# A two-layer attention and feed-forward kernel on one core: the feed-forward's first products leave PSUM through a 16-bit copy, and the order of segments and queries changes

## Chip, cores and metric

The kernel runs on one core of one Trainium2 chip. The time is device microseconds of one execution. The core has a matrix engine (TensorE, PE in the profile; its weight loads are PEld), a vector engine (VectorE, DVE), an activation engine (ScalarE, ACT), a general engine (GpSimd, POOL) and an engine that here only issues DMAs (SyncE, SP). Each engine works through its own instructions in the order in which the program lists them; semaphores hold an instruction until what it needs is done.

## The reference

```python
def _A_ref(x, wqkv, wo):            # B, S, D = 1, 2048, 512; H = 32 heads of 16
    qkv = (x @ wqkv).reshape(B, S, 3, H, Dh).transpose(2, 0, 3, 1, 4)
    q, k, v = qkv[0], qkv[1], qkv[2]
    p = _softmax(einsum("bhqd,bhkd->bhqk", q, k) * Dh ** -0.5, axis=-1)
    o = einsum("bhqk,bhkd->bhqd", p, v)
    return o.transpose(0, 2, 1, 3).reshape(B, S, D) @ wo

def _B_ref(x, w1, w2):              # w1 512 x 1792, w2 1792 x 512
    return silu(x @ w1) @ w2

x = x + _A_ref(_layernorm(x), A_wqkv, A_wo)
x = x + _B_ref(_layernorm(x), B_w1, B_w2)
x = x + _A_ref(_layernorm(x), A_wqkv, A_wo)      # the same weights again
x = x + _B_ref(_layernorm(x), B_w1, B_w2)
```

All tensors are bfloat16. The 2 x 32 softmaxes over 2048 x 2048 scores hold most of the work.

## The kernel before

**Tiles.** A layer's attention is cut into segments: a chunk c of 512 queries (4 chunks) by a head block hb of 4 heads (8 blocks). A segment of kind "all" goes over 16 key tiles of 128 keys, with two score tiles per key tile (a pair of heads each, 128 keys x 2 x 512 queries), 2048 score tiles in the whole program. In layer 1 the first segments are split: "old" segments take the first 12 key tiles, as the last chunk of layer 0 is not ready yet, and "new" segments the last 4; their partial sums are joined with a factor exp of the difference of the two shifts (`f_piece`, L465 and L468).

**A score tile's way.** TensorE makes it (L1209) in one of three PSUM slots of 1024 columns. Then one of two routes is taken. ScalarE applies the exponential (L1424, one instruction of 128 x 1024) and writes a bf16 buffer; one row for the value product. Or VectorE makes the bit pattern of a power of two by one multiply and add (L1454), and three further shifted versions of it come from integer adds, mostly on GpSimd (L1515), some on VectorE (L1488); the four together make four rows for the value product, whose sum stands for the exponential. TensorE multiplies rows with the values (L1285) into one PSUM bank per segment. A ones column beside the values gives the softmax's denominator. The row buffers are 11 tiles of its own and tiles lent from other tensors while these are idle: 12 more at the start, of which the last goes back at segment 32, and 12 again from segment 59.

**Side work.** Keys, queries, values, output projection, feed-forward and layer norms are "pieces": lists of steps (engine, planned ns, function, marks). All products of pieces go through one PSUM bank (tag "g", `narrow`). The mark "o" on a step opens that bank, "c" closes it: until the closing step's planned end no other piece may open it. "l" marks VectorE steps that are planned around GpSimd's running instruction (`self.lock`). Key pieces: 4 matmuls (L282, each as four column groups), copy (L291). Query pieces: 4 matmuls, copy (L359), absolute value (L366), bound times key maximum (L374), one matmul, sum (L383). The first product of the feed-forward, for each of 14 blocks of 128 hidden columns in each of 7 chunks: 4 matmuls into the bank, tanh of half of it on ScalarE into an fp32 tile (L545, `h_tanh`), and `(tanh + 1) * product` on VectorE with the product read from PSUM (L549, `h_out`), which closes the bank. Then four second products of 14 matmuls each, and the sum with x (L558). The eighth chunk's feed-forward is in `ending`, after the last segment, written out by hand.

**The planner.** `Flow` runs when the program is built. It keeps a planned time for each engine, takes the turn of the engine that is earliest, and lists the next instruction there; the order of all engines is so fixed before the run. `segs` is the order of segments. `musts(i)` gives what has to be made while segment i runs (`prep` of segment i+1 up to `n_old` = 41, of i+2 from there on), `due` gives it a due tile, `pace` a rate of credit that side pieces spend. `self.cur` is the one piece that holds the bank; `self.bg` are steps behind, which VectorE takes when it is free. `want_dve` decides whether VectorE gets a score tile: it needs, among other conditions, `SPARE` free row buffers beyond those owed, and not too many shifts waiting. `MANY` is the number of waiting row pairs above which value products go ahead of side work. `warm` lists idle matmuls (L1320) where TensorE has nothing else. `heads_piece` transposes a finished segment's output by DMA on the SP queue, two head blocks to a normalisation (L479, L480), one where it stands alone.

Of the kernel before, what the change touches and what calls it, by code (L numbers as in the profile page):

```python
# [20 lines left out]
def kernel(  # L21
# [10 lines left out]
    nc = tc.nc  # L32
# [25 lines left out]
    ) / 128  # L58
    BASE = 128 * (127 - MEAN)

    OLD = 3 * TT // 4
    MM, T_TANH, T_ISSUE, T_LAND, T_POOL = 217, 478, 1450, 2700, 2500
    NB = 11
# [168 lines left out]
    def pe(ns, fn, g=""):  # L232
        return ("pe", ns, fn, g)
# [218 lines left out]
    def f_piece(seg, after):  # L452

        cell = {}

        def a():
            cell["ps"] = narrow("f_ps")
            mm(cell["ps"][:, :], sel[:, 0, :], seg.QT, True, False)

        def b():  # L460
            mm(cell["ps"][:, :], sel[:, 1, :], q_kept(seg), False, True)

        def e():
            cell["f"] = tpool.tile([P, 512], FP32, name="f_sb", tag="t")
            nc.scalar.activation(cell["f"][:], cell["ps"][:, :], ACT.Exp, scale=float(SCALE))  # L465

        def m():
            nc.vector.tensor_tensor(  # L468
                out=o_kept(seg), in0=o_kept(seg), in1=cell["f"][:], op=ALU.mult
            )  # L470
            seg.scaled = True

        return Piece([pe(MM, a, "o"), pe(MM, b), act(T_TANH, e, "c"), dve(690, m, "l")], after)


    def heads_norm(at_ps, hb, attn):
# [10 lines left out]
    at_cell = {}  # L487

    def heads_piece(oT, seg, attn):
        alone = seg.L == 1 and (seg.c < 2 or (seg.c == NQC - 1 and seg.hb == HB - 2))  # L490
        k = 0 if alone else seg.hb % 2
        if k == 0:
            at_cell["at"] = opool.tile([P, 4, 2, P], BF16, name="at", tag="at")
        at = at_cell["at"]
        turn(at[:, :, k, :], oT[:])
        if not alone and k == 0:
            return None
        n = 4 * (k + 1)
        heads = at[:].rearrange("p t s (j w) -> p t (s j) w", j=4)[:, :, 0:n, :]
        return Piece([dve(640 if k == 0 else 920, lambda: heads_norm(heads, seg.hb - k, attn))])  # L500
# [64 lines left out]
    def ffn_pieces(c, emit_out, ln, after):  # L565
        cell = ln
        pieces = ln_pieces(c, ln, after)
        for ft in range(FT):
            hc = {}

            def a(ft=ft, hc=hc):
                bank(hc, "h_ps")

            def d(hc=hc):
                hc["t"] = h_tanh(hc["ps"][:, :])

            def e(ft=ft, hc=hc):
                h_out(cell["hT"], ft, hc["ps"][:, :], hc["t"])

            pieces.append(Piece(  # L580
                four(lambda cts, ft=ft, hc=hc: h_mm(c, ft, hc["ps"][:, :], cts), a)
                + [act(T_TANH, d), dve(690, e, "c")],
                pieces[1] if ft == 0 else None,
            ))
        for tq in range(4):
            yc = {}

            def ya(ft, tq=tq, yc=yc):
                if ft == 0:
                    bank(yc, "y2_ps")  # L590
                y_mm(cell["hT"], tq, yc["ps"][:, :], (ft,))

            def yb(tq=tq, yc=yc):
                y_out(4 * c + tq, yc["ps"][:, :], emit_out)

            pieces.append(Piece(
                [pe(MM, lambda ft=ft, ya=ya: ya(ft), "" if ft else "o") for ft in range(FT)]
                + [dve(690, yb, "c")] + ([] if emit_out else [stats_step(ln, c, tq)])
            ))
        return pieces  # L600

# [149 lines left out]
            self.opened = [False, False]  # L751

    segs = [Seg(0, c, hb, "all") for c in range(NQC) for hb in range(HB)]
    segs += [Seg(1, 0, hb, "old") for hb in range(HB)]
    segs += [Seg(1, 1, hb, "old") for hb in MORE]
    for hb in range(HB // 2):
# [18 lines left out]
        return pieces  # L775

    period = [c for c in range(NQC) for _ in range(HB)]
    period += [NQC] * (HB + len(MORE)) + [NQC + 1] * (2 * HB) + [NQC + 2] * (2 * HB)

    def ns_of(pieces):  # L780
# [48 lines left out]

    def musts(i):  # L830

        ts = list(range(i + 1 if i <= n_old else i + 2, i + 2 if i < n_old else i + 3))
        if (segs[i].L, segs[i].c) == (0, NQC - 2):
            ts.append(i + HB)
        last = (NQC - 1) * HB
        return [
            p for t in ts if t < len(segs) and not (last <= t < last + HB and t != i + HB)
            for p in due(prep(t), first[t])
        ]
# [59 lines left out]
    class Flow:  # L899

        def __init__(self):
            self.pe = self.act = self.dve = self.pool = self.sp = self.end = 0.0
            self.lock = self.held_port = 0.0
            self.mode = ""
            self.n = 0
            self.slots = [wide("slot") for _ in range(3)]
            self.free = [0.0] * 3
            self.held = [None] * 3
            self.exps = []
            self.zs = []  # L910
            self.passes = []
            self.lanes = [[], []]
            self.bufs = [(0.0, b) for b in bufs]
            self.retired = []
            self.qs = [[], [], [], []]
            self.cur = None
            self.bg = []
            self.g = 0.0
            self.credit = self.rate = 0.0
            self.open = 0  # L920
            self.o_ps = q_ps
            self.o_free = 0.0
            self.close_at = None
            self.last_dve = -9
            self.started = -1
            self.lost = 0.0
            self.runs = []
            self.heads = None
            self.chain = None
            self.units = [(tq, k) for tq in range(4) for k in range(CT)]  # L930
            self.kept = []
            self.turned = None
            self.log = {}
# [52 lines left out]
        def ready(self, p):  # L986
            at = p.ready
            if p.chain is not None and self.chain is not None and p.chain is not self.chain:
                return None
            for d in p.after:  # L990
                if not d.done:
                    return None
                at = max(at, d.ready)
            if "o" in p.steps[0][3]:
                at = max(at, self.g)
            return at

        def step(self, p, at):

            engine, ns, fn, g = p.steps.pop(0)  # L1000
            if not p.begun and p not in self.bg:
                self.cur = p
                for q in self.qs:
                    if p in q:
                        q.remove(p)
# [22 lines left out]
            fn()  # L1028
            if p.steps:
                p.land = max(p.land, self.landed(end))  # L1030
            if g == "c":
                self.g = end + 50
                self.cur = None
                if p.steps:
                    self.bg.append(p)
            if p.steps:
                p.ready = end + lat[("pe", "dve", "act").index(p.steps[0][0])]
            else:
                p.done = True
                if p.chain is not None and p.chain["last"] is p:  # L1040
                    self.chain = None
                p.ready = max(p.land, self.landed(end), end + 50 + p.lag)
                if p in self.bg:
                    self.bg.remove(p)
# [1 line left out]
        def front(self, pieces):  # L1046
            self.qs[0][:0] = pieces

        def background(self):
            return next((p for p in self.bg if self.ready(p) is not None), None)  # L1050

        def force(self, piece):
            while not piece.done:
                self.head()
                p = self.cur or self.background()
                if p is None:
                    q = next(q for q in self.qs if piece in q)
                    p = q[0]
                    if self.chain is not None and p.chain not in (None, self.chain):
                        self.force(self.chain["last"])  # L1060
                        continue
                    if p.steps[0][0] == "sp" or self.ready(p) is None:
                        self.force(next(d for d in p.after if not d.done))
                        continue
                at = self.ready(p)
                self.step(p, max(at, getattr(self, p.steps[0][0])))
# [340 lines left out]
        def act_turn(self):  # L1407
            t = self.act
            p = self.head()
            if p is not None and p.steps[0][0] == "act" and p.ready <= t + 150:  # L1410
                self.step(p, max(t, p.ready))
                return True
            if not self.exps:
# [125 lines left out]
    SWITCH, T_PASS, T_BITS, T_SHIFT = 100, 1225, 430, 1000  # L1539
    HELP, WAIT = 2, 100  # L1540

    LAST, BEHIND, SPARE, ROWS, LATE, EVEN = 5, 3, 5, 20, 900, 0
    SPAN, WARM, FEW, MANY = 3300, 0.65, 2, 8
    TAU, NEAR, URGENT, HARD = 700, 300, 4000, 6000
    FROM, TO, EARLY = 0, 99, 300
    EARLIER = 12
    HOT = 0.9
    MOST = 2600

    ordered = {  # L1550
# [153 lines left out]
```

## Time and profile before

| | us |
|---|---|
| median of 3 runs | 1661.9 (1661.09 to 1665.58) |
| the profiled execution's own time | 1662.01 |
| its span, first to last instruction | 1660.1 |
| granted TensorE clock, mean | 0.991 |
| busy: PE, ACT, POOL, DVE | 1576.4, 1592.1, 1220.3, 1152.4 |

The span is what the profile shows; 1.9 us of the execution lie around it. Busy time of an engine is the union of its instructions' spans. ScalarE's and TensorE's instructions overlap with their successors, so a mean duration there is longer than the distance from one start to the next. A group's row gives count, busy us, mean ns, then the idle time of that engine just before the group's instructions and what ended it.

### The profile page before, as it was taken

To read this page: it belongs to the slowest core of one execution; us is meant where nothing else is said; L and a number is where in the kernel's file an instruction comes from. 1 tells how busy PE (TensorE), PEld (TensorE's weight loads), DVE (VectorE), ACT (ScalarE), POOL (GpSimd) and SP (SyncE) were. 2 spreads that over 40 slices of the span, in tenths; PEclk is the share of its full clock that TensorE was granted. 3 is DMA by queue.
4 is the path that set the end of the run, shared out by engine and by line. 5 is a ranking of instruction groups with operands and counts; after the bars stand their busy time and mean duration, and the time that the engine had idled before them with its cause. 6 is when DMAs were issued, how large, how long until landed. Compare 5 with 4: busy or idle time off the path is not lost.

```text
span 1660.1 us, 42534 instructions
## 1 busy us (share of the span) xinstructions
PE 1576.4 (95%) x17499; PEld 503.8 (30%) x17505; DVE 1152.4 (69%) x1461; ACT 1592.1 (96%) x1805; POOL 1220.3 (74%) x1296
## 2 busy tenths in 40 slices
PE   7999999999999999999999998999999999999998
PEld 3232322233323333233232233222223222332333
DVE  6678779777877666656885557876665677687654
ACT  5899999999999999999999998999999999999993
POOL 2699998888788767767676655886567889788770
PEclk9999999999999999999999999998999999999999
DMA  5000000001000001000000000001000100010010
GB/s 190 5 8 8 5 20 21 8 5 21 21 21 5 8 21 30 8 8 18 21 14 2 2 14 8 11 11 30 17 8 11 27 21 8 15 36 8 11 24 13
DMA packets 83683, 30.79 MB, mean 19 GB/s; under 512 B 75552, under 2 KB 82464, under 8 KB 83488
## 3 DMA queue, kind: packets, MB, share of 16 engines
q1 hardware_dynamic: 82000, 26.10, 6.6%
q8 instruction: 137, 2.24, 0.6%
q10 hardware_dynamic: 1488, 1.97, 0.4%
q14 instruction: 58, 0.48, 0.1%
HBM read 7.86 MB, written 2.10 MB: 6 GB/s over the span
## 4 chain that ended last, share of the span: by engine, by line
PE 62%; ACT 21%; DVE 10%; issue 4%; POOL 1%; DMA 1%; ACTq 0%; DVEq 0%; POOLq 0%
PE slot L1209 21%; PE q_ps L1285 18%; ACT p L1424 13%; PE y_ps L282 7%; PE q_ps L282 4%; ACT v L1424 3%; PE k_ps L282 3%; PE h_ps L282 3%; ACT t_sb L545 3%; DVE p L1454 2%; DVE hT L549 1%; PE v_ps L282 1%; ACT q_old L1424 1%; PE q_ps L1320 1%; DVE attn L480 1%
## 5 line engine op out<-in xcount | busy, mean ns | idle before, releaser
L1424 ACT ACTIVATE p<-slot 128x1024 bf16<-128x1024 f32 x1173 | 1177.8, 1203 | 22.0 <-PE slot L1209 18.7
L1515 POOL TENSOR_TENSOR p<-p,steps 128x512 int32<-128x512 int32 x564 | 590.5, 1069 | 256.6 <-DVE p L1454 206.3
L1285 PE MATMUL q_ps<-p,v 128*17 128x512 bf16 x4594 | 532.8, 385 | 4.8 <-DVE p L1454 2.0
L1209 PE MATMUL slot<-QT,KT 32*128 32x512 bf16 x3104 | 443.0, 384 | 26.0 <-ACT p L1424 12.4
L1454 DVE TENSOR_SCALAR p<-slot 128x1024 uint16<-128x1024 f32 x280 | 341.6, 1220 | 127.0 <-PE slot L1209 119.8
L1209 PEld LDWEIGHTS <-KT 32*128 32x128 bf16 x4096 | 189.5, 91 | 587.1 <-issue 582.3
L1424 ACT ACTIVATE v<-slot 128x1024 bf16<-128x1024 f32 x306 | 350.6, 1233 | 2.0 <-PE slot L1209 2.0
L1285 PEld LDWEIGHTS <-v 128*17 128x17 bf16 x6586 | 165.8, 89 | 281.8 <-issue 223.5
L1285 PE MATMUL q_ps<-v,v 128*17 128x512 bf16 x1304 | 200.5, 381 | 1.9 <-DVE oT L1113 0.9
L1515 POOL TENSOR_TENSOR p<-v,steps 128x512 int32<-128x512 int32 x158 | 166.0, 1068 | 34.0 <-DVE v L1454 34.0
L1454 DVE TENSOR_SCALAR v<-slot 128x1024 uint16<-128x1024 f32 x99 | 121.0, 1222 | 66.0 <-PE slot L1209 62.8
L1515 POOL TENSOR_TENSOR v<-p,steps 128x512 int32<-128x512 int32 x133 | 141.1, 1068 | 30.6 <-DVE p L1454 27.2
L1424 ACT ACTIVATE q_old<-slot 128x1024 bf16<-128x1024 f32 x127 | 150.5, 1225 | 1.3 <-PE slot L1209 1.3
L282 PE MATMUL h_ps<-xnT,w_sb 128*32 128x512 bf16 x1568 | 130.5, 384 | 14.0 <-DVE hT L549 11.8
L1209 PE MATMUL slot<-q_old,KT 32*128 32x512 bf16 x896 | 121.3, 382 | 5.5 <-ACT p L1424 4.8
L549 DVE SCALAR_TENSOR_TENSOR hT<-t_sb,h_ps 128x512 bf16<-128x512 f32 x98 | 67.0, 684 | 79.0 <-ACT t_sb L545 79.0
L282 PE MATMUL y_ps<-w_sb,hT 128*32 128x512 bf16 x1568 | 119.4, 383 | 0.9 <-DVE qc L359 0.3
L1285 PE MATMUL q_ps<-q_old,v 128*17 128x512 bf16 x578 | 99.5, 381 | 0.5 <-DVE oT L1113 0.2
L282 PE MATMUL q_ps<-xnT,wkq 128*32 128x512 bf16 x1008 | 84.7, 384 | 2.9 <-DVE hT L549 1.2
L282 PE MATMUL k_ps<-xnT,wkq 128*32 128x512 bf16 x960 | 80.5, 388 | 2.5 <-DVE KT L291 1.4
L1515 POOL TENSOR_TENSOR q_old<-p,steps 128x512 int32<-128x512 int32 x67 | 72.2, 1085 | 11.4 <-DVE p L1454 11.2
L1515 POOL TENSOR_TENSOR v<-v,steps 128x512 int32<-128x512 int32 x63 | 67.3, 1075 | 13.4 <-DVE v L1454 12.2
(162 smaller groups left out, 1512.3 us busy)
## 6 DMA issues: line engine op xcount, KB each, us to landing
w_sb<-in_B_w_dram SPq DMA_DIRECT2D x2, 1792.0 KB, 14.7
out_dram<-x_sb SPq DMA_DIRECT2D x15, 128.0 KB, 1.7
x_sb<-in_A_x_dram SPq DMA_DIRECT2D x3, 512.0 KB, 10.3
wraw<-in_A_wqkv_dram ACTq DMA_DIRECT2D x1, 1024.0 KB, 8.4
at<-oT SPq DMA_TRANSPOSE x63, 2.3
xnT<-hT SPq DMA_TRANSPOSE x44, 2.3
wv_sb<-in_A_wqkv_dram ACTq DMA_DIRECT2D x1, 512.0 KB, 10.7
wo_sb<-in_A_wo_dram SPq DMA_DIRECT2D x1, 512.0 KB, 11.3
```

Of the source, the lines that this page charges most:

```text
L282: nc.tensor.matmul(ps[g, :], lhsT=lhsT[:, g], rhs=rhs, start=start, stop=stop, skip_group_check=True)
L480: nc.vector.tensor_tensor(out=attn[:, :, 64 * hb : 64 * hb + DH * n].rearrange("p t (j d) -> p t j d", j=n), in0=at_ps[:, :, :, 0:DH], in1 ...
L545: nc.scalar.activation(t_sb, ps, ACT.Tanh, scale=0.5)
L549: nc.vector.scalar_tensor_tensor(out=hT[:, ft, :], in0=t_sb, scalar=1.0, in1=ps, op0=ALU.add, op1=ALU.mult)
L1209: nc.tensor.matmul(self.slots[k][:, jj, :], lhsT=KT[32 * j : 32 * j + KR, t.seg.hb, t.kt * P : (t.kt + 1) * P], rhs=t.seg.QT[32 * j : 32 * ...
L1285: nc.tensor.matmul(self.o_ps[32 * j : 32 * j + VW, :], lhsT=vs[seg.L][:, t.kt, 4 * seg.hb + j, :], rhs=buf[:, jj, :], start=not seg.opened ...
L1320: nc.tensor.matmul(out[0:DH, :], lhsT=wkq[rows, 0, 2 * D : 2 * D + DH], rhs=wo_sb[rows, 0, :], start=out is not self.o_ps, stop=out is not ...
L1424: nc.scalar.activation(buf[:].rearrange("p a b -> p (a b)"), self.slots[x.slot][:].rearrange("p a b -> p (a b)"), ACT.Exp, scale=float(SCALE),
L1454: nc.vector.tensor_scalar(out=whole.bitcast(U16), in0=self.slots[x.slot][:].rearrange("p a b -> p (a b)"), scalar1=float(UNIT), scalar2=fl ...
L1515: nc.gpsimd.tensor_tensor(out=b1.bitcast(I32), in0=b0.bitcast(I32), in1=steps32[:, k : k + 1].to_broadcast([P, 512]), op=ALU.add,)
```

## The change

The feed-forward's product in the seven planned chunks goes from PSUM to SBUF by a VectorE copy into its place in `hT` (bf16), which closes the bank; tanh and product read that copy, the product writes over it in place. Tanh and product are now background steps, with a mark "t" so that one tanh tile is in use at a time, and ScalarE's turn looks among background steps. The second products wait for all fourteen first ones. Segment (chunk 1, head block 0) moves to second place, behind (chunk 0, head block 0); the heads of blocks 0 and 1 of chunks 0 and 1 are normalised alone. From segment 16 on queries are prepared two segments ahead. `SPARE` goes from 5 to 4 and `MANY` from 8 to 6. The ending keeps its own order and reads PSUM as before.

```diff
-        return Piece([pe(MM, a, "o"), pe(MM, b), act(T_TANH, e, "c"), dve(690, m, "l")], after)
+        return Piece([pe(MM, a, "o"), pe(MM, b), act(T_TANH, e, "ct"), dve(690, m, "l")], after)
...
-        alone = seg.L == 1 and (seg.c < 2 or (seg.c == NQC - 1 and seg.hb == HB - 2))
+        alone = seg.c < 2 and (seg.L == 1 or seg.hb < 2)
+        alone = alone or (seg.L, seg.c, seg.hb) == (1, NQC - 1, HB - 2)
...
-            def d(hc=hc):
-                hc["t"] = h_tanh(hc["ps"][:, :])
+            def w(ft=ft, hc=hc):
+                nc.vector.tensor_copy(out=cell["hT"][:, ft, :], in_=hc["ps"][:, :])
+
+            def d(ft=ft, hc=hc):
+                hc["t"] = h_tanh(cell["hT"][:, ft, :])
 
             def e(ft=ft, hc=hc):
-                h_out(cell["hT"], ft, hc["ps"][:, :], hc["t"])
+                h_out(cell["hT"], ft, cell["hT"][:, ft, :], hc["t"])
 
             pieces.append(Piece(
                 four(lambda cts, ft=ft, hc=hc: h_mm(c, ft, hc["ps"][:, :], cts), a)
-                + [act(T_TANH, d), dve(690, e, "c")],
+                + [dve(690, w, "c"), act(T_TANH, d, "t"), dve(T_PROD, e)],
                 pieces[1] if ft == 0 else None,
             ))
+        hs = pieces[2:]
...
-                + [dve(690, yb, "c")] + ([] if emit_out else [stats_step(ln, c, tq)])
+                + [dve(690, yb, "c")] + ([] if emit_out else [stats_step(ln, c, tq)]), hs
             ))
...
     segs = [Seg(0, c, hb, "all") for c in range(NQC) for hb in range(HB)]
+    segs.insert(1, segs.pop(HB))
...
     period = [c for c in range(NQC) for _ in range(HB)]
+    period[HB] = 0
...
     def musts(i):
 
-        ts = list(range(i + 1 if i <= n_old else i + 2, i + 2 if i < n_old else i + 3))
+        ts = [i + 1] * (i <= AHEAD) + [i + 2] * (i >= AHEAD)
+        if n_old < AHEAD + HB * 5 and n_old - 2 <= i <= n_old + 1:
+            ts = {n_old - 2: [n_old], n_old - 1: [], n_old: [n_old + 1], n_old + 1: [n_old + 2, n_old + 3]}[i]
...
+            if "t" in p.steps[0][3] and self.t_user is not None:
+                return None
...
+            if "t" in g:
+                self.t_user = p
...
-            if g == "c":
+            if "c" in g:
...
                 p.done = True
+                if self.t_user is p:
+                    self.t_user = None
...
-        def background(self):
-            return next((p for p in self.bg if self.ready(p) is not None), None)
+        def background(self, engines=("dve",)):
+            able = [p for p in self.bg if p.steps[0][0] in engines and self.ready(p) is not None]
+            now = [p for p in able if self.ready(p) <= getattr(self, p.steps[0][0]) + 150]
+            return now[0] if now else min(able, key=self.ready, default=None)
...
-                p = self.cur or self.background()
+                p = self.cur or self.background(("dve", "act"))
...
-            if p is not None and p.steps[0][0] == "act" and p.ready <= t + 150:
+            if p is None or p.steps[0][0] != "act" or self.ready(p) is None:
+                p = self.background(("act",))
+            if p is not None and p.ready <= t + 150:
...
-    LAST, BEHIND, SPARE, ROWS, LATE, EVEN = 5, 3, 5, 20, 900, 0
-    SPAN, WARM, FEW, MANY = 3300, 0.65, 2, 8
+    LAST, BEHIND, SPARE, ROWS, LATE, EVEN = 5, 3, 4, 20, 900, 0
+    SPAN, WARM, FEW, MANY = 3300, 0.65, 2, 6
...
+    AHEAD = 16
+    T_PROD = 690
```

More of the change, by code (lines that the diff above doesn't have):

```diff
@@ L1039, in step @@
                 p.done = True
+                if self.t_user is p:
+                    self.t_user = None
                 if p.chain is not None and p.chain["last"] is p:
@@ L1547 @@
     HOT = 0.9
+    AHEAD = 16
+    T_PROD = 690
     MOST = 2600
```

## The prediction

> **What bounds the kernel now.** I began with the page's header, busy shares and slices, to find the engine that never pauses.
>
> ```profile
> span 1660.1 us, 42534 instructions
> PE 1576.4 (95%) x17499; PEld 503.8 (30%) x17505; DVE 1152.4 (69%) x1461; ACT 1592.1 (96%) x1805; POOL 1220.3 (74%) x1296
> ACT  5899999999999999999999998999999999999993
> ```
>
> Two engines stand near the full span. ScalarE (ACT) is below 9 in four slices only: the first, the last, the second (41 to 83 us) and the 25th (996 to 1037 us). The matmul share is less telling, for single matmuls of 384 ns overlap, and the groups hold filler (181 of L1320 into q_ps alone), which the scheduler adds only where TensorE has nothing else. So the sum is made on ScalarE. Next came the groups, for the price of each operation.
>
> ```profile
> L1424 ACT ACTIVATE p<-slot 128x1024 bf16<-128x1024 f32 x1173 | 1177.8, 1203 | 22.0 <-PE slot L1209 18.7
> L545 ACT ACTIVATE t_sb<-h_ps 128x512 f32<-128x512 f32 x98 | 74.5, 760 | 0.0
> L549 DVE SCALAR_TENSOR_TENSOR hT<-t_sb,h_ps 128x512 bf16<-128x512 f32 x98 | 67.0, 684 | 79.0 <-ACT t_sb L545 79.0
> L468 DVE TENSOR_TENSOR v<-v,f_sb 128x512 f32<-128x512 f32 x8 | 9.6, 1194 | 4.2 <-ACT f_sb L465 4.2
> ```
>
> The four tile names of L1424 (p, v, q_old, idle) sum to 1173 + 306 + 127 + 27 = 1633 exponentials; the other 415 of the 2048 score tiles go to VectorE (L1454: 280 + 99 + 30 + 6). ScalarE's operations overlap, so the price of one is start to start. In the timeline eight exponentials fill 429.45 to 436.77 us: 0.91 us each. A tanh starts at 501.67 and the next exponential at 502.15: 0.48 us. Then 1633 x 0.91 + 98 x 0.48 + 10 rescaling exponentials x 0.48 = 1538 us, against 1580 us from the first exponential (37.6) to the end of the last one's turn (about 1617). Some 42 us are gaps; 43 us lie behind the last one, in the ending, which is not touched.
>
> Then the timeline, for where the gaps are. The largest:
>
> ```profile
> 65.28 0.29 DVE L374 TENSOR_SCALAR bm<-E,amax 128x128 bf16<-128x128 f32 x1
> 66.55 0.40 PE L282 MATMUL q_ps<-qu,bm 128*32 128x512 bf16 x4
> 67.00 0.69 DVE L383 TENSOR_TENSOR QT<-q_ps,qc 128x512 bf16<-128x512 f32 x1 [1.44 <-PE q_ps L282]
> 67.74 0.61 PE L1209 MATMUL slot<-QT,KT 32*128 32x512 bf16 x6 [0.79 <-DVE QT L383]
> 68.17 2.86 ACT L1424 ACTIVATE p<-slot 128x1024 bf16<-128x1024 f32 x3 [5.73 <-PE slot L1209]
> ```
>
> ScalarE idles 5.73 us at the end of the first segment: scores of the second need its query QT, which needs the key maximum of head block 1, whose last key copy ends at 64.3. Within 37 to 76 us the excess over the usual spacing is 9.8 us. A second cluster lies at 985 to 1161 us, where the new keys of the second layer arrive: 18 gaps, 15 us together, the longest 1.9. Elsewhere there is next to nothing: from 93 to 565 us ScalarE is busy 470.66 of 472 us.
>
> Last, VectorE's share of the exponentials by stage, and the waits around the bank that the change frees:
>
> ```profile
> 93.00:565.00 472.00, 173.19 (x142) 1.00 0.06 13
> 565.00:1008.00 443.00, 118.51 (x97) 1.00 0.06 13
> 1233.00:1594.00 361.00, 129.44 (x106) 1.00 0.08 18
> ```
>
> ```profile
> DVE hT L549 <- ACT t_sb L545: 79.0, 65, 2.7
> PE h_ps L282 <- DVE hT L549: 11.8, 29, 0.7
> ```
>
> VectorE takes 0.30, 0.22 and 0.29 tiles per us. The weak middle is where the lent buffers have gone back (14, then 12 and 11 tiles instead of 23). The single projection bank costs TensorE 11.8 us of waits behind the feed-forward product, never over 0.7 at a time, in stretches where ScalarE does not stop.
>
> **The change, part by part.**
>
> *Order of segments.* Segment 1 becomes (chunk 1, head block 0), whose keys exist; it needs one query (4 matmuls of one piece, four VectorE steps). Head block 1's keys get all of segment 1, where 84 column matmuls fitted into 25 us before. Of the 9.8 us I keep the first 0.95 (start-up) and some 0.8 for a new boundary: -8. Bounds -10 and -4 (the key chain is late for segment 2 instead). The two heads left unpaired add two normalisations of 0.86 + 0.25 us in place of half of two of 1.13 + 0.35: about 1.5 us of VectorE, hidden. Their transposes on SP are as many as before.
>
> *Freeing the bank.* A copy ends the hold of the bank, before it lasted over the tanh's turn on ScalarE and the product. By the waits above this gives ScalarE nothing: 0 by itself. It lets the feed-forward of chunk 3 end sooner, ahead of 985 to 1161; with the queries there re-timed I take -3 of those 15 us, bounds -8 and +3 (segment 43's query is now queued a segment later). The second products wait for all 14 first ones: up to a tanh's turn (0.9 + 0.48) and a product (1.2) per chunk, 2.6 x 7 = 18 us in the feed-forward's own queue; other queues' pieces fill TensorE, and ScalarE waits only where a due time is missed: 0.
>
> *Queries two segments ahead from segment 16.* Between segments 16 and 40 boundaries show no gap over 1.3 us, most none: 0.
>
> *SPARE 5 to 4, MANY 8 to 6.* One buffer less is held back when VectorE is offered a tile. From 14 buffers (418 to 565 us: 39 tiles, 0.265 per us) to 11 or 12 (0.22) the rate falls by about 0.02 per us for one buffer. Over the 700 us that are short of buffers (418 to 1008 and 1151 to 1260) this would be 14 tiles x 0.91 = 13 us. The reserve was also there for ScalarE's own buffers, so I take half: -7, bounds -14 and +2. MANY works on long lists of waiting rows, which 11 buffers do not hold: 0.
>
> *VectorE's added work.* 98 copies from PSUM at 0.69 (as L341, 691 ns) = 68 us. The product now has both inputs in SBUF. The rows nearest to it are L468 and L480, also with two:
>
> ```profile
> 1019.22 3.21 POOL L1515 TENSOR_TENSOR p<-p,steps 128x512 int32<-128x512 int32 x3 [4.76 <-DVE p L1454]
> 1021.45 1.52 DVE L468 TENSOR_TENSOR v<-v,f_sb 128x512 f32<-128x512 f32 x1
> ```
>
> GpSimd's running shift ends at 1022.43, and VectorE's operation 0.54 us after that: it had waited 0.98. All ten of L468 last as long as the running shift has left, and about 0.55 more. So a product costs about 1.19 instead of 0.684, 98 x 0.5 = 50 us more, and the scheduler counts it as 690 ns without a turn on the port. Together VectorE gains 118 us, 69% to 76%. The cover is its idle time, 31% of the span. Where that fails, a tile goes back to ScalarE. Bounds 0 and +19 (a quarter of the 118 displaces tiles of 1.22 + 0.2 us: 21 x 0.91); I take +5. Queued behind a late product stand key and query copies and passes that free score slots. From 93 to 565 us many VectorE operations already wait for GpSimd (L366 lasts 735 ns on the mean, 278 at the least) and ScalarE lost 1.3 us: +3, bounds 0 and +10.
>
> *The tanh's source*, SBUF in 16 bits instead of PSUM. No wide ScalarE operation here reads SBUF. Of its 0.48 us, 0.43 go with the 512 elements (0.91 less 0.48); the fixed 0.05 might vanish or double: 98 x 0.05 = 5 us either way; I take 0, as both rows have the same fixed part. [...]
>
> Sum: -8 - 3 - 7 + 5 + 3 = -10 us. The profiled execution took 1662.0 us (span 1660.1 and 1.9 around it), the median of the runs is 1661.9: forecast 1652.
>
> **The rivals.**
>
> *VectorE pays in tiles (slower), 0.21.* In the feed-forward segments of the buffer-rich stages (273 to 350, 1329 to 1426) VectorE is 78 and 75% busy and GpSimd 86 and 89%; up to five products and copies add 5 x 1.19 = 6 us to 24. If a quarter of the 118 us displaces tiles, +19, and the spare buffer then brings nothing; with -8 - 3 it is +8: 1670. It turns slower where displaced work passes a seventh (11 of 76 us). For it: the product's price is underrated by the scheduler. Against: 28 of the 98 products fall between 565 and 1008 us, where VectorE is 65% busy.
>
> *Gain and price cancel, 0.16.* The start's 8 us come, the tanh from SBUF (+5) and the delays (+3) take them back, tiles stay: 1662.
>
> *Buffers were the bound, 0.19.* The middle's rate rises half-way, to 0.26: 0.04 x 443 = 18 tiles there, 5 in other short stretches, 23 x 0.91 = 21 us, with 11 from the gaps and 8 of costs: 1638.
>
> **How the numbers follow.** My forecast has 0.44. About 0.3% (5 us) is what a measurement of this kernel can tell from no change. Faster is the forecast and the buffer case, 0.63; same 0.16; slower 0.21. The range goes from the buffer case to the slower rival: 1638 to 1670; beyond both lie some 2 in 10.
>
> **What would show it.** Right: no ScalarE gap over 2 us between 60 and 70 us; 1620 to 1640 exponentials on L1424's counterpart (under 1620 is the buffer case); the product at 1.1 to 1.2 us mean; tanh to the next exponential still 0.48; VectorE at 75 to 77%. Wrong: more than 1640 exponentials (VectorE pays), the same 5 us gap one segment later, or single-microsecond ScalarE gaps spread over the feed-forward segments.

## The result, and the profile after

The changed kernel is slower, by half a per cent: median 1671.4 us (ten runs, 1665.6 to 1677.2) against 1662.5 us for the kernel before on the same chips (ten runs, 1661.1 to 1665.6); ratio 1.0052, interval [1.0036, 1.0067]. The forecast was 1652, faster. The granted clock explains a part at most: the two runs of the changed kernel at 0.992 took 1667.6 and 1669.5 us, and the kernel before took 1660.9 to 1663.6 at that clock in its runs beside the experiments. In this part the segments are numbered from 0, "excess" is ScalarE's time from one operation's start to the next beyond the usual 0.904 us of an exponential, and a "shift" is GpSimd's operation on the score tiles that VectorE has passed (L1536). Line numbers differ a little from kernel to kernel.

The page of the profiled execution (1671.08 us), the same three lines as before:

```profile
span 1669.3 us, 42739 instructions
PE 1584.4 (95%) x17540; PEld 506.5 (30%) x17540; DVE 1245.5 (75%) x1555; ACT 1592.7 (95%) x1798; POOL 1292.3 (77%) x1332
ACT  5999999999999999999999999999999999999993
```

VectorE went from 69 to 75% and GpSimd from 74 to 77%. ScalarE's two weak slices (the 2nd and the 25th) are 9 now, and yet the span is 9 us longer: no new slice is weak, so the loss is spread thin.

ScalarE's timeline at the end of the first segment, where it idled 5.73 us before (columns: start, busy time, engine and line, operation, count; a wait would stand in brackets):

```profile
58.83 1.06 ACT L1445 ACTIVATE v<-slot 128x1024 bf16<-128x1024 f32 x1
59.73 3.82 ACT L1445 ACTIVATE p<-slot 128x1024 bf16<-128x1024 f32 x4
63.34 1.12 ACT L1445 ACTIVATE v<-slot 128x1024 bf16<-128x1024 f32 x1
64.25 1.14 ACT L1445 ACTIVATE p<-slot 128x1024 bf16<-128x1024 f32 x1
```

The gap is gone and did not come back a segment later. The groups of the feed-forward steps, and the costliest of ScalarE (busy and mean ns, then idle time ahead of them and what ended it):

```profile
L1445 ACT ACTIVATE p<-slot 128x1024 bf16<-128x1024 f32 x1163 | 1148.6, 1167 | 18.0 <-PE slot L1228 15.8
...
L551 DVE SCALAR_TENSOR_TENSOR hT<-t_sb,hT 128x512 bf16<-128x512 f32 x98 | 92.8, 947 | 20.3 <-ACT t_sb L547 20.0
...
L577 DVE CAST hT<-h_ps 128x512 bf16<-128x512 f32 x98 | 67.2, 686 | 26.2 <-PE h_ps L283 23.4
...
L547 ACT ACTIVATE t_sb<-hT 128x512 f32<-128x512 bf16 x98 | 65.7, 671 | 13.1 <-DVE hT L551 10.8
```

The product (L551) grew from 684 to 947 ns, and the tanh, which never idled before, idles 13.1 us. The waits (releaser, total us, count, longest):

```profile
ACT t_sb L547 <- DVE hT L551: 10.8, 22, 1.3
...
PE q_ps L1304 <- POOL p L1536: 10.3, 21, 1.2
...
PE q_ps L1304 <- POOL q_old L1536: 3.4, 5, 1.1
PE h_ps L283 <- DVE hT L577: 2.0, 4, 1.1
```

TensorE's wait for the bank fell from 11.8 us to 2.0. Now ScalarE waits for the products, because one t_sb buffer carries every tanh, and TensorE's value matmuls (L1304) wait 13.7 us for GpSimd's shifts. Each wait is about a microsecond. One feed-forward step shows both:

```profile
501.20 1.31 POOL L1536 TENSOR_TENSOR v<-p,steps 128x512 int32<-128x512 int32 x1 [0.76 <-ACT p L1445]
...
501.53 1.52 DVE L551 SCALAR_TENSOR_TENSOR hT<-t_sb,hT 128x512 bf16<-128x512 f32 x1
...
502.47 1.48 POOL L1536 TENSOR_TENSOR p<-p,steps 128x512 int32<-128x512 int32 x1
...
503.15 0.63 ACT L547 ACTIVATE t_sb<-hT 128x512 f32<-128x512 bf16 x1 [1.06 <-DVE hT L551]
...
503.69 1.01 ACT L1445 ACTIVATE p<-slot 128x1024 bf16<-128x1024 f32 x1
```

The product is issued at 501.53 while a shift runs. The shift ends at 502.51 and the product 0.54 us later, at 503.05. The next shift was issued at 502.47, while the product still ran, and lasts 1.48 us: it ends 0.90 us after the product. So do all 88 shifts that are issued while one of these products runs (0.89 to 0.90 us after it), and they last 1470 ns on the mean; before, with the product's second tensor in PSUM, the 37 shifts issued while a product ran lasted 1049. The next tanh cannot write t_sb until the product has read it: 1.06 us of idle ScalarE.

**Where the 9 us went**, in the two profiled executions, by the starts of ScalarE's operations. The last exponential starts 9.2 us later (1616.28, now 1625.49).

| part | before | after | us |
|---|---|---|---|
| exponentials on ScalarE, at 0.904 | 1633 | 1626 | -6.3 |
| excess in segments 0 and 1 | 10.0 | 3.0 | -7.0 |
| excess in segments 41 to 55, the layer change | 17.4 | 11.2 | -6.2 |
| excess in all other segments | 24.9 | 48.2 | +23.4 |
| 98 tanh steps, start to next start | 477 ns | 533 ns | +5.5 |
| sum | | | +9.4 |

So the change earns 19.5 us and loses 29. The 23.4 us lie in the feed-forward segments: where tanh steps run, the excess went from about 12 us to about 37, and in the rest of these other segments it stayed at about 12. The question for the runs is what the 23.4 us are.

### The profile page after: what moved, and what is told of

The parts are those of the page before. It is cut to its first block, busy times and chain, and to the rows that moved or that the text cites. A ratio compares the mean times of both kernels' runs of the same rounds, so it can differ in the third digit from the quotient of the medians.

```text
span 1669.3 us, 42739 instructions
## 1 busy us (share of the span) xinstructions
PE 1584.4 (95%) x17540; PEld 506.5 (30%) x17540; DVE 1245.5 (75%) x1555; ACT 1592.7 (95%) x1798; POOL 1292.3 (77%) x1332
## 5 line engine op out<-in xcount | busy, mean ns | idle before, releaser
L1445 ACT ACTIVATE p<-slot 128x1024 bf16<-128x1024 f32 x1163 | 1148.6, 1167 | 18.0 <-PE slot L1228 15.8
L1536 POOL TENSOR_TENSOR p<-p,steps 128x512 int32<-128x512 int32 x604 | 651.5, 1101 | 222.1 <-DVE p L1475 188.0
L1304 PE MATMUL q_ps<-p,v 128*17 128x512 bf16 x4634 | 536.1, 384 | 15.9 <-POOL p L1536 10.3
L1228 PE MATMUL slot<-QT,KT 32*128 32x512 bf16 x3104 | 450.3, 383 | 27.0 <-ACT p L1445 14.2
L1475 DVE TENSOR_SCALAR p<-slot 128x1024 uint16<-128x1024 f32 x294 | 358.7, 1220 | 134.4 <-PE slot L1228 116.5
L1304 PEld LDWEIGHTS <-v 128*17 128x17 bf16 x6628 | 166.6, 89 | 310.6 <-issue 252.1
L1304 PE MATMUL q_ps<-v,v 128*17 128x512 bf16 x1312 | 202.5, 382 | 1.8 <-POOL v L1536 0.8
L1536 POOL TENSOR_TENSOR v<-p,steps 128x512 int32<-128x512 int32 x146 | 159.9, 1102 | 29.1 <-DVE p L1475 22.5
L1536 POOL TENSOR_TENSOR p<-v,steps 128x512 int32<-128x512 int32 x132 | 142.4, 1096 | 26.2 <-DVE v L1475 25.5
L1475 DVE TENSOR_SCALAR v<-slot 128x1024 uint16<-128x1024 f32 x77 | 93.8, 1219 | 20.4 <-PE slot L1228 18.2
L551 DVE SCALAR_TENSOR_TENSOR hT<-t_sb,hT 128x512 bf16<-128x512 f32 x98 | 92.8, 947 | 20.3 <-ACT t_sb L547 20.0
L1304 PE MATMUL q_ps<-q_old,v 128*17 128x512 bf16 x572 | 94.8, 382 | 3.5 <-POOL q_old L1536 3.4
L577 DVE CAST hT<-h_ps 128x512 bf16<-128x512 f32 x98 | 67.2, 686 | 26.2 <-PE h_ps L283 23.4
L547 ACT ACTIVATE t_sb<-hT 128x512 f32<-128x512 bf16 x98 | 65.7, 671 | 13.1 <-DVE hT L551 10.8
## 6 DMA issues: line engine op xcount, KB each, us to landing
wv_sb<-in_A_wqkv_dram ACTq DMA_DIRECT2D x1, 512.0 KB, 10.8
```

The costliest lines, as they stand in the source:

```text
L547: nc.scalar.activation(t_sb, ps, ACT.Tanh, scale=0.5)
L551: nc.vector.scalar_tensor_tensor(out=hT[:, ft, :], in0=t_sb, scalar=1.0, in1=ps, op0=ALU.add, op1=ALU.mult)
L577: nc.vector.tensor_copy(out=cell["hT"][:, ft, :], in_=hc["ps"][:, :])
L1228: nc.tensor.matmul(self.slots[k][:, jj, :], lhsT=KT[32 * j : 32 * j + KR, t.seg.hb, t.kt * P : (t.kt + 1) * P], rhs=t.seg.QT[32 * j : 32 * ...
L1304: nc.tensor.matmul(self.o_ps[32 * j : 32 * j + VW, :], lhsT=vs[seg.L][:, t.kt, 4 * seg.hb + j, :], rhs=buf[:, jj, :], start=not seg.opened ...
L1445: nc.scalar.activation(buf[:].rearrange("p a b -> p (a b)"), self.slots[x.slot][:].rearrange("p a b -> p (a b)"), ACT.Exp, scale=float(SCALE),
```

## The experiments

Each was timed beside the kernel before, which took 1662.1 to 1662.9 us on these chips. Ratios are to that kernel. Edits are to the changed kernel unless said otherwise, and "..." in them stands for lines left out. A kernel whose costs, marks or settings are edited gets its instructions ordered anew by the scheduler. The four that only exchange the operands or the operation inside a step keep the changed kernel's order. Only where the order is kept does one step alone vary. In no_port and late_dve the product's multiplication is left out and the rest is computed.

**no_port: a product that reads one tensor.**

```diff
-                h_out(cell["hT"], ft, cell["hT"][:, ft, :], hc["t"])
+                nc.vector.tensor_reduce(
+                    out=cell["hT"][:, ft, :], in_=hc["t"].rearrange("p (f o) -> p f o", o=1),
+                    axis=AX.X, op=ALU.max,
+                )
```

> The changed kernel with one edit: the feed-forward product (tanh + 1) * copy is replaced by a VectorE reduction over an axis of length one that reads the tanh tile alone (one SBUF input, no two-input read; it leaves the multiplication out), planned at the same 690 ns, so the listed order stays. Theory A (the product has two SBUF inputs and waits for GpSimd's running shift, which the planner does not know, and the lateness reaches ScalarE): the instruction falls from 947 to about 690 ns mean, the waits of tanh on the product (10.8 us in the planned chunks) and most of the short score waits in the feed-forward segments go, 12 to 20 us faster than the changed kernel: 1651 to 1659. Theory B (the amount of VectorE work, 98 more copies, is what delays): within 4 us of the changed kernel's 1671. Theory C (planner settings): also 1671.

Measured: 1644.6 us (1643.1 to 1648.3), ratio 0.989 [0.9873, 0.9907]; 26.8 us under the changed kernel, and more than theory A expected. Its group and waits:

```profile
L583 DVE TENSOR_REDUCE hT<-t_sb 128x512 bf16<-128x512 f32 x98 | 66.5, 679 | 21.7 <-ACT t_sb L547 21.7
```

```profile
PE q_ps L1307 <- POOL p L1539: 1.3, 5, 0.4
...
ACT t_sb L547 <- DVE hT L583: 1.0, 4, 0.4
```

With the same list of instructions, the same 1626 exponentials and the same 1173 shifts, both waits almost vanish (10.3 to 1.3, 10.8 to 1.0) and the excess falls from 62.4 to 39.0 us, by 23.4, as much as had appeared in the feed-forward segments. The copies and the settings are still there, so theories B and C are out: the whole loss, and more, hangs on the product. Part of the 26.8 us goes with the granted clock, which was 0.995 to 0.997 in four of the five runs and 0.985 to 0.994 in the changed kernel. The fifth run, the profiled one, had 0.992 and took 1648.3 us, 20 under the changed kernel at 0.992. Why the clock differs was not tested.

**late_dve: the lateness without the second tensor.** Reductions of one tensor, of 512 and 1024 elements in turn, mean 945 ns, where the product takes 947.

```diff
-                h_out(cell["hT"], ft, cell["hT"][:, ft, :], hc["t"])
+                one = hc["t"].rearrange("p (f o) -> p f o", o=1)
+                nc.vector.tensor_reduce(
+                    out=cell["hT"][:, ft, :], in_=one if ft % 2 else one.to_broadcast([P, 512, 2]),
+                    axis=AX.X, op=ALU.max,
+                )
```

> The changed kernel with the product replaced by one-input reductions of the tanh tile (the multiplication is left out): over 512 elements in every second block, over 1024 in the others, so that the mean of one is about 0.95 us as the product's was (947 ns), in the same listed order and planned at 690, but without a second SBUF input. If the lateness on VectorE itself is what costs (theory V: what stands behind it in VectorE's queue): 1660 to 1671, near the changed kernel. If the shifts that the product holds up on GpSimd cost, and TensorE's value products behind them (theory G: shifts across a product lasted 1307 ns instead of 1053): 1645 to 1653, near the 1644.6 of the kernel with short one-input reductions.

Measured: 1658.8 us, ratio 0.9976 [0.9968, 0.9985].

```profile
L584 DVE TENSOR_REDUCE hT<-t_sb 128x512 bf16<-128x1024 f32 x49 | 59.4, 1211 | 7.6 <-ACT t_sb L547 7.6
...
L584 DVE TENSOR_REDUCE hT<-t_sb 128x512 bf16<-128x512 f32 x49 | 33.3, 679 | 14.5 <-ACT t_sb L547 14.0
```

```profile
ACT p L1449 <- PE slot L1232: 10.9, 13, 2.4
...
ACT t_sb L547 <- DVE hT L584: 8.8, 22, 0.8
...
PE q_ps L1308 <- POOL p L1540: 1.7, 6, 0.4
```

The time lies between the ranges of theories V and G: the 26.8 us are of two halves. VectorE being late costs 14.2 (1658.8 less 1644.6): the tanh's wait is back at 8.8. Holding up GpSimd costs the other 12.6 (1671.4 less 1658.8): with nothing in GpSimd's way the value matmuls wait 1.7 us instead of 10.3, and ScalarE waits 10.9 us for slots (p<-slot) instead of 15.8. The split is good to a few us: the lateness was matched on its mean and not step by step. Runs at the same granted clock, 0.992, split the same way: the changed kernel 1668.5 (mean of two), late_dve 1658.8 (median of three), no_port 1648.3 (one run), so some 10 us each.

**two_tiles: every second tanh into another tile**, so that it need not wait for the product before it.

```diff
-                hc["t"] = h_tanh(cell["hT"][:, ft, :])
+                if ft % 2 == 0 and ft < FT - 2:
+                    t2 = cell["hT"][:, FT - 2 : FT, :].bitcast(FP32).rearrange("p a b -> p (a b)")
+                    hc["t"] = h_tanh(cell["hT"][:, ft, :], t2)
+                else:
+                    hc["t"] = h_tanh(cell["hT"][:, ft, :])
```

> The changed kernel with the same listed order, but every second tanh (blocks 0, 2 to 10) writes to another place (the still unused last two blocks of hT), so a tanh no longer waits for the product before it. Theory A with the single tanh tile as the way by which the lateness reaches ScalarE: the tanh's waits on the product (about 15 us with their restarts) nearly go, 8 to 15 us faster: 1656 to 1663. Theory A with the lateness going through TensorE and the score slots: under 4 us. Theories B and C: no change, 1671.

Measured: 1668.8 us, ratio 1.0032 [1.002, 1.0044]; 2.6 us under the changed kernel, with intervals that overlap.

```profile
ACT p L1449 <- PE slot L1232: 13.7, 16, 2.4
PE q_ps L1308 <- POOL p L1540: 13.6, 26, 1.2
...
ACT t_sb L547 <- DVE hT L551: 5.0, 7, 1.0
...
ACT v L1449 <- PE slot L1232: 4.1, 7, 1.0
ACT q_old L1449 <- PE slot L1232: 4.1, 4, 1.6
```

The edit moves 42 of the 98 tanh results and takes away about half of the tanh's wait (10.8 to 5.0 us). Against these 5.8 us, ScalarE waits 2.8 more for score slots (21.9 in the three rows shown, 19.1 in the changed kernel), and the value matmuls wait longer for the shifts (13.6 against 10.3). So the one t_sb buffer is a small part as far as this goes; what a second buffer for every tanh would bring is not shown.

**t16: the tanh's result in 16 bits**, so that all of the product's operands are.

```diff
-                hc["t"] = h_tanh(cell["hT"][:, ft, :])
+                t16 = tpool.tile([P, 512], BF16, name="t16", tag="t")[:]
+                hc["t"] = h_tanh(cell["hT"][:, ft, :], t16)
```

> The changed kernel with the tanh's result in 16 bits instead of 32, in the same listed order; the product then reads 2 + 2 bytes per element instead of 4 + 2. If the product holds the port for less time with 16-bit inputs (theory: half, about 0.3 us instead of 0.57): products of 0.68 us mean, shifts across it shorter, 8 to 14 us faster, 1657 to 1663. If its speed does not depend on the type: 1671 within 3 us.

Measured: 1669.3 us, ratio 1.0036 [1.0022, 1.005], not told apart from the changed kernel.

```profile
L551 DVE SCALAR_TENSOR_TENSOR hT<-t,hT 128x512 bf16<-128x512 bf16 x98 | 95.1, 970 | 20.3 <-ACT t L547 20.0
```

The shortest product takes 675 ns, as with 32 bits, and the mean of 970 is no shorter than the 947 there: the narrower type does not speed it.

**priced and planned: the scheduler is told.** First the price alone, then the mark "l" on the product, by which the scheduler plans its turn against GpSimd's shifts.

```diff
-    T_PROD = 690
+    T_PROD = 950
```

```diff
-                + [dve(690, w, "c"), act(T_TANH, d, "t"), dve(T_PROD, e)],
+                + [dve(690, w, "c"), act(T_TANH, d, "t"), dve(T_PROD, e, "l")],
```

> The changed kernel with the planner's price for the product at 950 ns, its measured mean, instead of 690. If the cost comes from the order not knowing the price: 3 to 12 us faster, 1660 to 1668. If the cost is the port itself, or the feed-forward's longer plan misses its due times as it did in the kernel with the mark l: within 4 us of 1671, or slower.

> The changed kernel with the mark l on the product's step, so that the planner puts it behind GpSimd's running shift and holds GpSimd's next one until it ends. Everything is computed. Theory A1 (the loss is that the order does not know of the port, so that a product lies across a shift and makes shift and product late): products fall to about 0.7 us mean, shifts lying across a product become few, the waits of value matmuls on GpSimd (13.7 us against 1.3 without the two-input read) go, and the time nears the kernel without it: 1645 to 1655. Theory A2 (98 products on the port take away from GpSimd whatever the order): shift time saved is lost as idle time of GpSimd, and the time stays within 5 us of 1671.

Measured: priced 1694.4 us, ratio 1.0185 [1.017, 1.02]; planned 1702.4, ratio 1.0244 [1.023, 1.0258]. Both are worse than leaving the price wrong. ScalarE at the layer change, in the waits of priced (990 to 1030 us) and the timeline of planned:

```profile
ACT p L1445 <- PE slot L1228: 15.4, 1, 15.4
```

```profile
1023.04 1.94 ACT L1445 ACTIVATE p<-slot 128x1024 bf16<-128x1024 f32 x2 [6.04 <-PE slot L1228]
```

The new orders bring the second layer's keys late: the last sum of chunk 3's feed-forward (L560) ends at 997.8 and 993.1 us, in the changed kernel at 982.2, and ScalarE stands in one wait of 15.4 us and one of 6.0. That is about half of priced's loss and less of planned's. The excess of priced is 14.6 us higher in segments 41 to 55 and 15.5 from segment 56 on; in planned it is 6.4 and 14.5, and 12 more exponentials run on ScalarE (1638). The granted clock was lower too (0.982 to 0.986 and 0.977 to 0.981), and what that costs here was not tested. In planned the products still take 986 ns, and 68 of the 98 still start while a shift runs (79 in the changed kernel). The scheduler's price of a shift is not the plain reason: it counts 1000 ns (T_SHIFT), and a shift that the next one follows at once takes 997 from start to start in the median (1037 is how long one lasts). Why the planned turns are missed stays open.

**The parts on their own.** The new segment order alone, put into the kernel before; the old segment order in the changed kernel; the old query times in the changed kernel. The edit of order_back is the first one below turned round:

```diff
...
     segs = [Seg(0, c, hb, "all") for c in range(NQC) for hb in range(HB)]
+    segs.insert(1, segs.pop(HB))
...
```

```diff
-        ts = [i + 1] * (i <= AHEAD) + [i + 2] * (i >= AHEAD)
...
+        ts = list(range(i + 1 if i <= n_old else i + 2, i + 2 if i < n_old else i + 3))
```

> The kernel before with the new order of segments alone (chunk 1 head block 0 second, heads of blocks 0 and 1 of chunks 0 and 1 normalised alone). All theories: the 5.7 us gap at 62 us goes; 5 to 8 us faster than before: 1654 to 1657. If 1662 or more, the start's gain is lost later in the plan and does not depend on the feed-forward's copy.

> The changed kernel with the old order of segments (and the old pairs of heads), all the rest as changed. By the prediction's first step: 6 to 8 us slower, 1677 to 1680, with the 5 us gap at 62 us back. If the start's gain is taken back at the layer change, as in the kernel with the new order alone: within 4 us of 1671.

> The changed kernel with the rule of before for when queries are made (one segment ahead, and its old rule around the layer change). By the prediction's step (queries cost and bring nothing but a re-timing worth 3 us around the layer change): 1668 to 1678. If the layer change is missed, as it was by 41 us of idle time in the kernel without the copy: 1685 or more.

Measured: order_only 1667.8 us, ratio 1.003 [1.002, 1.004], 5 us slower than before; order_back 1687.3, ratio 1.0147 [1.0133, 1.0161], 16 slower than the changed kernel; queries_back 1674.8, ratio 1.0079 [1.0065, 1.0093], 3.4 slower than it, with intervals that only touch. In order_only segment 2 starts 6.6 us ahead of the kernel before, segment 38 only 0.6 ahead, and segment 41 starts 7.4 behind: what is left is lost just ahead of the layer change, in segments 38 to 40 (excess 11.2 us, before 0.6). ScalarE's waits around there, first of order_only (925 to 1032 us), then of the kernel before (925 to 1026):

```profile
ACT p L1427 <- PE slot L1212: 16.1, 5, 3.9
```

```profile
ACT p L1424 <- PE slot L1209: 4.6, 5, 1.5
```

Of order_back's 16 us, 8.3 are excess in segments 0 and 1, the forecast's size, and 9.6 lie at the layer change (segments 41 to 55). So the start's gain is real, and whether it reaches the end depends on how the plan comes out 900 us later. Which due times do it was not followed further.

**The copy and the settings apart.** copy_only has the copy, its marks and the background rule in the kernel before, and nothing else. no_copy is the changed kernel with the feed-forward's product and tanh on PSUM as before; its second products still wait for all fourteen. rules_back undoes the two reserve settings.

```diff
...
-                + [act(T_TANH, d), dve(690, e, "c")],
+                + [dve(690, w, "c"), act(T_TANH, d, "t"), dve(T_PROD, e)],
...
```

```diff
...
-                h_out(cell["hT"], ft, cell["hT"][:, ft, :], hc["t"])
+                h_out(cell["hT"], ft, hc["ps"][:, :], hc["t"])
...
-                + [dve(690, w, "c"), act(T_TANH, d, "t"), dve(T_PROD, e)],
+                + [act(T_TANH, d, "t"), dve(690, e, "c")],
```

```diff
-    LAST, BEHIND, SPARE, ROWS, LATE, EVEN = 5, 3, 4, 20, 900, 0
-    SPAN, WARM, FEW, MANY = 3300, 0.65, 2, 6
+    LAST, BEHIND, SPARE, ROWS, LATE, EVEN = 5, 3, 5, 20, 900, 0
+    SPAN, WARM, FEW, MANY = 3300, 0.65, 2, 8
```

> The kernel before with the feed-forward's copy alone (copy, background tanh and product, second products behind all fourteen); order of segments, queries, SPARE 5 and MANY 8 as before. Theory A alone (price of the product, some 23 us, and the tanh's 5.5): slower than before by 10 to 30 us, 1672 to 1692, as nothing else pays it back. Theory D (the copy ends the feed-forward sooner, which the layer change needs, and so pays part back): 1655 to 1672.

> The changed kernel with the feed-forward as before (tanh and product read PSUM, the product closes the bank), all the rest (order, queries ahead, SPARE 4, MANY 6, background turn of ScalarE) as changed. Theories A and B (copy or product is the loss): 1645 to 1655. Theory C (the settings are the loss): 1665 or more.

> The changed kernel with SPARE 5 and MANY 8 as before. If the two numbers gave the 7 fewer exponentials and the rest does not depend on them: 633 or more of 2048 tiles less on VectorE (exponentials back to 1630 to 1640), 4 to 10 us slower than the changed kernel, 1675 to 1681. If their more shifts are what collides with the products: 3 to 10 us faster, 1661 to 1668.

Measured: copy_only 1682.4 us, ratio 1.0121 [1.0107, 1.0135]; no_copy 1692.8, ratio 1.0179 [1.0159, 1.0199]; rules_back 1683.7, ratio 1.0133 [1.011, 1.0156], with 1632 exponentials. rules_back is slower than either of its expectations. no_copy lands where theory C put it, but C is not the reason, for no_port keeps the settings and takes 1644.6. It breaks mainly at one place (ScalarE's timeline, then VectorE's):

```profile
1000.89 8.63 ACT L1442 ACTIVATE p<-slot 128x1024 bf16<-128x1024 f32 x9
1043.76 2.85 ACT L1442 ACTIVATE p<-slot 128x1024 bf16<-128x1024 f32 x3 [34.24 <-PE slot L1225]
```

```profile
1039.49 0.81 DVE L292 TENSOR_SCALAR KT<-k_ps,cols 128x512 bf16<-128x512 f32 x1 [1.15 <-PE k_ps L283]
...
1042.53 0.69 DVE L443 TENSOR_TENSOR QT<-q_ps,q_old 128x512 bf16<-128x512 f32 x1 [0.99 <-PE q_ps L283]
```

Here the feed-forward of chunk 3 ends so late that its keys are copied at 1039.5 and the query at 1042.5, and ScalarE stands still for 34 us. The last of its first products ends at 977.2 us, in the changed kernel at 945.9. Most of this was there before it began: its first tanh runs at 890.4, against 865.6. The bank is held longer without the copy, but it is not shown that this alone makes the plan late; the kernel before holds it in the same way and ends these products at 944.6. The two halves of the change belong together: from 1662.5, the copy alone adds 20 us, the rest alone adds 30, and both add 9. That is some 41 less than their sum. A price for each edit by itself can't give that number.

## Why the prediction was wrong

**The failed step is "VectorE's added work", booked at +8** (5 for tiles, 3 for delays). The product's own price was roughly foreseen: 1.19 us was too high (79 products that start while a shift runs took 1010 ns on the mean, the other 19 took 683, all together 947), and VectorE's 75% is near the 76% expected. What failed is the conversion of that price into time. No tile was displaced: VectorE passed 422 instead of 415. The delays cost 23.4 us of excess and, against a product with one tensor, 26.8 us of time: at the same granted clock about 20: the upper bound of +10 for them was far too low. The sum without this term is -18, so 1644, and no_port took 1644.6. That meeting is partly luck. In its profiled run (1648.3 us) the exponentials and the excess in segments 0 and 1 and in 41 to 55 do sum to -18, but the tanh costs 4.7, which the sum had at 0, and the median lies lower because the other runs had a higher granted clock.

Two readings led there. "The cover is its idle time, 31% of the span" takes a mean busy share for cover. The listed order is fixed: while the product waits, what follows it on VectorE stands still, and an idle microsecond later does not pay that back. And the stretch from 93 to 565 us, where "many VectorE operations already wait for GpSimd" and ScalarE lost 1.3 us, was taken as proof that such delays are harmless. It shows only that the delays which that order already had were harmless. The prediction then followed what stands behind the product on VectorE and forgot the other party, GpSimd. late_dve and no_port together show what that party costs, 12.6 of the 26.8 us. The path is read from the traces' waits: a held-up shift delays the value matmuls in TensorE's listed order (10.3 us against 1.7), these delay the scores behind them, and ScalarE waits for a slot (15.8 us against 10.9). The last link has no run of its own.

**The slower rival** had nearly the right time (1670) with the wrong mechanism: tiles did not go back to ScalarE. Its reason, a price that the scheduler underrates, is half right: the underrating is a fact (690 ns planned, 947 measured), but priced and planned, in which the scheduler is told, took 23 and 31 us more than the kernel in which it is not. The third of the signs named for a wrong forecast, single-microsecond gaps spread over the feed-forward segments, is the one that came: 0.3 to 3.5 us of excess in each, over 0.9 in 19 of the 22.

**Order of segments**, -8: measured -7.0 in segments 0 and 1. Right there, but order_only shows that it does not stand alone. The prediction put all gaps at 42 us; with 0.904 us for an exponential instead of 0.91 they come to 52.

**Freeing the bank and re-timing the layer change**, -3: measured -6.2, inside its bounds. "0 by itself" for the bank is not settled: no_copy, without it, stalls 34 us, but its feed-forward was late before it began, and the kernel before has no such stall. What the runs show is that the copy and the rest of the change can't be priced apart, so the bank's short waits were no safe measure of its worth.

**SPARE and MANY**, -7: seven exponentials fewer, -6.3 us. Undoing them gave 1632, six more, and 12 us, half of it by the count. **Queries**, 0: worth 3.4 us when undone, near what can be told.

**The tanh's source**, 0 with ±5: measured +5.5, just past the upper end. From SBUF a tanh takes 533 ns to the next start instead of 477. There are two steps: about 520 ns (45 of the 98, all issued while ScalarE's operation before them still ran) and about 536 (52); one holds a wait and took 988. The argument that both rows have the same fixed part could not carry the 0: the rows that 0.91 and 0.48 come from (L1424 and L545) both read PSUM. From there the same 512 elements take 43 ns more in the shorter step and 56 more on the mean of all 98. Whether that lies in a fixed part is not shown, for all 98 have one size.

**Faster by what?** No kernel here that computes everything beat the one before. no_port's 1644.6 shows what the change would be worth (18 us) if the product could be made without a second tensor from SBUF; no run here does this and still multiplies, and part of the 18 us goes with that run's higher granted clock (14 at 0.992).

## What to carry to other kernels

Before an operand is moved from PSUM to SBUF, look at what GpSimd does at that time: here a product of two SBUF tensors that met a running shift ended about 0.55 us after that shift, the next shift 0.90 us after the product, and the delays travelled along in-order queues to ScalarE (10.8 us of waits) and TensorE (13.7). An engine's mean idle share (VectorE's was 25% here) is no measure of cover in an order that is fixed in advance; count the operations that can be late, and follow who is queued behind them on every engine, until the one that sets the time. In a kernel whose settings were fitted together, undoing one part prices the misfit along with the part, so compare kernels with the same order of instructions where you can.

## What the runs showed of the hardware

- A product of two SBUF tensors, 128x512, takes 683 ns where no shift runs at its start (19 of the 98). Otherwise it takes what the shift has left and about 0.55 us more (correlation of time left and time taken 0.94 over the 98; the few that start with under 0.1 us left take 681 ns). Before, with one of the two tensors in PSUM, it took 685 ns on the mean where a shift ran at its start (81 of 98) and 682 where none did.
- Shifts that a product of two SBUF tensors lies across last 1307 ns on the mean; before, with the product's second tensor in PSUM, shifts across it lasted 1053. The runs show these times and not what makes the engines wait: the "port" of the prediction and the expectations is a name from the scheduler (`held_port`). What surprised was the price: with 98 such products 26.8 us of 1671 (about 20 at the same granted clock), almost half of it through GpSimd.
- A tanh of 512 elements costs ScalarE 477 ns start to start from PSUM (32 bits) and about 520 or 536 ns from SBUF (16 bits), 533 on the mean.
- 16-bit operands throughout do not shorten VectorE's product: the shortest takes 675 ns with them and with a 32-bit one, the mean is 970 against 947.
